# A planned instruction order with refitted prices, whole PSUM tiles as the unit, and another place for the last layer's sums

## The chip, the cores and the metric

The kernel runs on one core of one Trainium2 chip. The core has five engines that run side by side: TensorE (PE) for matmuls, VectorE (DVE), ScalarE (ACT), GpSimd (POOL) and SyncE (SP), which here issues nearly all transfers. Matmuls write PSUM, which has eight banks; everything else lies in SBUF. The metric is the time of one execution on the device in microseconds: 832.44 us is the median of three runs before the change (832.07 to 832.96).

## The reference

The input is q, k, v of 4 batches, 8 heads, 768 tokens and 64 features, and a projection of 64 to 6. Each query and key gets a bucket from the signs of its six projections, and attention is allowed only inside a bucket. The output of attention goes through a two-layer feed-forward net with the activation relu squared.

```python
def _attn_ref(q, k, v, proj):
    q_bits = (np.einsum('bhsd,dk->bhsk', q, proj) > 0)   # k_bits alike
    q_bucket = np.sum(q_bits * powers, axis=-1)
    mask = q_bucket[:, :, :, None] == k_bucket[:, :, None, :]
    scores = np.where(mask, scale * np.matmul(q, k.transpose(0, 1, 3, 2)), -1e9)
    attn = np.exp(scores - np.max(scores, axis=-1, keepdims=True))
    attn = attn / (np.sum(attn, axis=-1, keepdims=True) + 1e-09)
    return np.matmul(attn, v)

def reference(...):                     # x: 3072 x 512
    h = np.maximum(x @ w_in, 0.0)       # w_in: 512 x 2048
    return h * h @ w_out                # w_out: 2048 x 512
```

## The kernel before, in words

**The work.** Numbers are split into two half-precision parts where accuracy needs it, so that one product becomes two or three matmuls. A visit is one batch, one pair of heads and one half (384) of the queries; there are 32. A visit has six units, one for each head and block of 128 queries. `unit` computes the scores pS of 128 queries against 768 keys on TensorE (the matmuls `pS<-A,Q` and `pS<-L,M`; the masks ride in extra rows of the operands), copies them to SBUF on DVE with their maximum (`e<-pS`), takes the exponential on ACT with the sum (`e<-e`), turns the sum into a factor rv (POOL or DVE, and a reciprocal on DVE), and writes the normalised rows as a high part on ACT and a low part on DVE (`hl`). A transposing DMA brings hl to aT. In the first four visits, the plain ones, e is scaled on POOL instead, transposed on TensorE into pT in 32-bit precision and copied out on ACT or DVE. `av` multiplies aT with the values V into pA, which is evicted as two parts xx.

`prep` makes the operands of a head pair: it loads R, splits it into A and L, computes the buckets (`pd`, `bits`, `pc`, M) and stacks the parts with copies inside SBUF (`Q<-L`, `Q<-A`, `A<-A`, `L<-M`, `M<-Q`). `first` does the same for the very first visit in another layout, with K and G loaded side by side and the masks MK and MG out of one PSUM tile pc of three banks.

When the four head pairs of a half of a batch are there, `moe` runs the two dense layers for its 384 tokens; there are eight such stages. For each of 16 slices of 128 hidden units it gathers pm (12 matmuls of 384 columns), evicts it through relu, square and a split into g (high and low part), and adds the slice to po: for each of three token blocks t, three matmuls of 512 columns. po is one PSUM tile of three banks, one for each block. After the last slice the three blocks are evicted into o and sent out. The weights arrive in 32 tiles `raw`, each of which is unpacked on ACT (`top`) and DVE (`f`) and split into win or wo. `verify` looks at the ranges of inputs and weights late in the program; if one were out of range, a second, general program would follow, which does not run here.

**What sets the order.** The functions do not emit instructions. They add operations to a planner, the class `Program`. An operation has one or several ways (engine and form), a rank, and the operations that it depends on. `region` says which part of a tile an operation touches, and `add` makes a dependency where two accesses overlap and at least one writes. For PSUM tiles `region` counts whole banks, so operations in different banks of one tile are independent for the planner. `cost` gives each way a time that the engine is taken and a time until the result is there; for transfers these come from fixed figures and a rate. `forward` then plays the program: at each step the engine that is free first takes the ready operation of best priority; `backward` derives new priorities from that plan, and the best of five plans by its own span is kept. `emit` hands the operations out in the order of this plan, so it fixes the order on every engine, and on SP's queue of transfers. What an instruction really waits for is set below the planner, by the framework that places semaphores from the tiles' accesses. The plan's times play no part on the chip, only its order does.

**Names and lines.** `TRANSPOSES` is the rate for transposing transfers; `TOP_BY`, `LOW_BY`, `RUN` and `ALTERNATE` steer smaller choices. `pS` has two banks, `po` three, `pA`, `pm` and `misc` one each: eight in all. In the profile nearly all instructions carry L427, the line in `emit` that issues single operations, and L424, the one that issues grouped matmuls; they are told apart by their tiles.

Of the kernel before, what the change touches and what calls it, by code (L numbers as in the profile page):

```python
# [23 lines left out]
P = 128  # L24
# [32 lines left out]

WIN_AT, WOUT_AT = (0, 2), 1
# [5 lines left out]
RUN = 18  # L64
CONSTS_BY, WIDE = ("sp", "sp", "sp"), 1
# [16 lines left out]
TRANSPOSES = 165  # L82
# [47 lines left out]
class Program:  # L130
# [25 lines left out]
    def region(view):  # L156
# [5 lines left out]
        if rec.kind == "psum":  # L162
            return 0, 1, f0 // 512, 1 + (f0 % rec.row + size(ap.ap[1:]) - 1) // 512, 0, 0, 0
# [5 lines left out]
    def add(self, *ways):  # L169
# [25 lines left out]
    def cost(key, name, args, kw):  # L195
# [16 lines left out]
        if name.startswith("dma"):  # L212
# [3 lines left out]
            return busy, b / (TRANSPOSES if name == "dma_start_transpose" else 314)  # L216
        if key == "act":
            t = 93 * (isinstance(kw.get("scale"), View) + isinstance(kw.get("bias"), View)) + (51 if "psum" in kinds[:2] else 93) + n / 1.2 + 93 * ("accum_out" in kw)
        elif key == "pool":
            t = 147 + n * (2.1 if args[0].dtype == F32 or args[0].dtype == F32R else 1.88) if name == "tensor_tensor" else 161 + n / 1.2 + 83 * ptr  # L220
        else:
            fast = name in ("tensor_copy", "tensor_scalar") and "psum" not in kinds[:2]
            both = len(args) > 3 and isinstance(args[3], View) and args[3].shape[-1] == 1
            t = 67 + 100 * ("accum_out" in kw) + n / (1.92 if fast else 0.96) + 62 * (ptr and (fast or name == "scalar_tensor_tensor")) + 100 * both
# [93 lines left out]
    def forward(self, prio, near):  # L318
# [7 lines left out]
        free = dict.fromkeys(keys, 0.0)  # L326
        out, dma, dge, held, kind = [], 0.0, 0.0, 0.0, None
# [11 lines left out]
        while True:  # L339
# [109 lines left out]
def run(ctx: ExitStack, tc, kq, v, proj2, w_in, w_out, consts, out, flag):  # L449
# [56 lines left out]
    if fast:  # L506
# [8 lines left out]
        codes = sb([P, 4 * P], BF16, "codes")  # L515
# [148 lines left out]
    def first(hp):  # L664

        K, G = [sb([P, n], F32, name, tag="VV") for name, n in (("K", S), ("G", HS))]
# [3 lines left out]
        MK, MG = sb([P, S], F16, "MK", tag="M"), sb([P, HS], F16, "MG", tag="Q")  # L670
        halves = K[:, 0:HS], K[:, HS:], G
        pd = ps([P, 512], F32, "pd", tag="misc")[:, 0:HS]
        matmuls(*[(pd[32 * n : 32 * n + 32], pj, x) for n, x in enumerate(halves)])
        bits = sb([P, HS], BF16, "bits")
        act.activation(bits[0:96], pd[0:96], AF.Sign, scale=2.0**60, bias=thr[0:96])
# [5 lines left out]
        pr.add((act, "activation", (MG, pc[:, 2], AF.Relu), {"bias": shift}), (dve, "tensor_scalar", (MG, pc[:, 2], 2.0**16, 0.0, ALU.subtract, ALU.max), {}))  # L681
        return K, G, MK, MG

    def side_by_side(st, half, i):

        K, G, MK, MG = st
        c0 = half * HS + i * P
# [51 lines left out]
    def unit(st, half, i, aT, plain, pS=None):  # L739
        c0 = half * HS + i * P  # L740
# [42 lines left out]
    def av(b, hp, half, VV, aTs):  # L783
        pA = ps([P, 512], F32, "pA")[:, 0:HS]
# [8 lines left out]
        xx = xxs[b, half, hp] = sb([P, 2, HS], F16, "xx")  # L793
# [13 lines left out]
    def moe(n, b, half):  # L807
        X = [xxs.pop((b, half, cc)) for cc in range(NCC)]
# [5 lines left out]
        for f in range(NF + 1):  # L814
            if f == NF // 2:
                pr.checked = len(pr.ops)
            if f < NF:
# [3 lines left out]
                for cc in reversed(range(NCC)):  # L821
                    pr.mark = pace()
                    wh = win[:, 0, cc, f * P : (f + 1) * P]
                    wl = win[:, 1, cc, f * P : (f + 1) * P]
                    pe.matmul(pm[:, 0:HS], wh, X[cc][:, 0], start=cc == NCC - 1, stop=False)
                    pe.matmul(pm[:, 0:HS], wh, X[cc][:, 1], start=False, stop=False)
                    pe.matmul(pm[:, 0:HS], wl, X[cc][:, 0], start=False, stop=cc == 0)
                pr.rank, pr.mark = RANK_MOE, None

                g32 = sb([P, HS], F32, "g32", 2)  # L830
                pr.add((act, "activation", (g32, pm[:, 0:HS], AF.Relu), {"scale": HS2 if fast else 2.0**-23}),
                       (dve, "tensor_scalar", (g32, pm[:, 0:HS], HS2 if fast else 2.0**-23, 0.0, ALU.mult, ALU.max), {}))
                square(g32, g32)
                g = gs[f] = sb([P, 2, HS], F16, "g")
# [3 lines left out]
            if f > 0:  # L838
# [4 lines left out]
                if first:  # L843
                    po = ps([P, 3, DM], F32, "po")
                for t in range(3):
# [3 lines left out]
                    pe.matmul(po[:, t], gh, wo[:, 0, m], start=first, stop=False)  # L849
                    pe.matmul(po[:, t], gh, wo[:, 1, m], start=False, stop=False)  # L850
                    pe.matmul(po[:, t], gl, wo[:, 0, m], start=False, stop=last)
# [6 lines left out]
                for t in range(3):  # L858
                    r0 = b * S + half * HS + t * P
                    if grouped and last:  # L860
                        if m == 3:
                            move(acc[:, t], po[:, t], back)
# [170 lines left out]
```

## Time and profile before

| | |
|---|---|
| median of three runs | 832.44 us |
| the profiled execution | 834.86 us |
| its span, first to last instruction | 833.1 us |
| TensorE busy | 794.3 us (95%) |
| ACT busy | 656.6 us (79%) |
| DVE busy | 605.2 us (73%) |
| POOL busy | 72.7 us (9%) |
| DMA, share of 16 engines' span on SP's queue | 77.2% |
| first matmul of a dense layer (pm) | 97.70 us |

The profile is of one execution, with times in us from the first instruction. Busy time of an engine is the union of its instructions. A wait row reads "who waited <- for whom: us in total, times, longest". A timeline row reads "start, duration, engine, line, operation, out<-in, shape, count, and in brackets the idle time before it and what ended it"; instructions of one kind that follow each other are merged into one row. A matmul's duration covers its way through the array, so that matmuls overlap; the step from one to the next is shorter than the duration.

### The profile page before, as it was taken

How to read it: one execution, taken by the hardware profiler on the slowest of the kernel's cores; microseconds unless marked ns; L12 is line 12 of the kernel's file. 1: busy time of each engine (PE TensorE's matmuls, PEld its weight loads, DVE VectorE, ACT ScalarE, POOL GpSimd, SP SyncE). 2: the span in 40 equal slices, each digit the busy share in tenths (PEclk: the TensorE clock that was granted, in tenths of full speed). 3: DMA queues.
4: the chain of work that ended last, by engine and by line, in shares of the span. 5: the costliest groups of instructions: out<-in, count | busy, mean ns of one | idle time of the engine just before them, and what ended most of it. 6: DMA issues, size and time to landing. Idle time of an engine off the chain costs nothing. (4 is left out here: it accounts for less than half of the span.)

```text
span 833.1 us, 14383 instructions
## 1 busy us (share of the span) xinstructions
PE 794.3 (95%) x5001; PEld 430.0 (52%) x5001; DVE 605.2 (73%) x1200; ACT 656.6 (79%) x1238; POOL 72.7 (9%) x175
## 2 busy tenths in 40 slices
PE   7797799999999999999999999999999999999996
PEld 4354355555555554555555545555555554555553
DVE  6888989998999888898879755888889433611110
ACT  5898999998888989888898856888988997334443
POOL 1255200100000010000000000000002000000000
PEclk9999999999999999999999999999999999999999
DMA  8985979999999999999989866988975889501001
GB/s 258 270 223 181 292 188 179 214 176 195 183 202 196 195 188 213 192 181 219 194 188 186 212 165 140 181 143 148 146 133 99 239 290 304 212 1 39 1 1 42
DMA packets 299521, 145.93 MB, mean 175 GB/s; under 512 B 268752, under 2 KB 279344, under 8 KB 299440
## 3 DMA queue, kind: packets, MB, share of 16 engines
q1 hardware_dynamic: 299440, 144.93, 77.2%
q8 instruction: 41, 0.67, 0.3%
q14 instruction: 40, 0.33, 0.1%
HBM read 56.80 MB, written 6.29 MB: 76 GB/s over the span
## 5 line engine op out<-in xcount | busy, mean ns | idle before, releaser
L427 PE MATMUL po<-wo,g 128*128 128x512 f16 x1152 | 296.9, 379 | 5.7 <-ACT o L427 5.7
L427 PE MATMUL pm<-xx,win 128*128 128x384 f16 x1536 | 297.7, 326 | 4.4 <-ACT g L427 2.8
L427 PEld LDWEIGHTS <-win 128*128 128x128 f16 x1536 | 149.9, 98 | 116.6 <-issue 8.0
L427 DVE TENSOR_SCALAR_CACHE_REDUCE e<-pS 128x768 f32<-128x768 f32 x192 | 182.7, 953 | 21.9 <-PE pS L427 17.7
L427 ACT ACTIVATE e<-e,maxes 128x768 f32<-128x768 f32 x192 | 178.2, 929 | 20.7 <-DVE e L427 19.2
L427 DVE SCALAR_TENSOR_TENSOR hl<-e,rv,hl 128x768 f16<-128x768 f32 x168 | 171.0, 1019 | 18.8 <-ACT hl L427 17.8
L427 PEld LDWEIGHTS <-g 128*128 128x128 f16 x1152 | 111.9, 98 | 124.8 <-issue 9.1
L427 ACT ACTIVATE hl<-e,rv 128x768 f16<-128x768 f32 x168 | 154.6, 923 | 6.0 <-DMA aT<-hl 5.2
L427 DVE SCALAR_TENSOR_TENSOR g<-g,g 128x384 f16<-128x384 f32 x121 | 66.9, 553 | 111.8 <-ACT g L427 111.4
L427 ACT ACTIVATE g<-g 128x384 f32<-128x384 f32 (+1 forms) x251 | 129.4, 517 | 6.6 <-PE po L427 2.7
L427 ACT ACTIVATE g<-pm 128x384 f32<-128x384 f32 x127 | 61.2, 482 | 90.3 <-PE pm L427 90.0
L427 PE MATMUL pS<-A,Q 128*128 128x384 f16 x372 | 93.1, 330 | 4.1 <-DVE e L427 2.6
L427 PE MATMUL pS<-L,M 128*128 128x384 f16 x372 | 91.8, 327 | 0.8 <-DMA M<-Q 0.8
L424 PE MATMUL pA<-aT,VV 128*64 128x384 f16 x1008 | 87.2, 327 | 0.0
L427 POOL TENSOR_SCALAR rv<-sums 128x1 f32<-128x1 f32 x136 | 36.8, 271 | 541.7 <-ACT e L427 400.2
L424 PEld LDWEIGHTS <-VV 128*64 128x64 f16 x1008 | 54.7, 110 | 32.9 <-issue 10.0
L427 PEld LDWEIGHTS <-Q 128*128 128x128 f16 x372 | 34.2, 98 | 43.1 <-issue 16.2
L427 DVE TENSOR_SCALAR M<-pc,masks 128x384 f16<-128x384 f32 x64 | 43.0, 672 | 15.4 <-PE pc L427 15.2
L427 PEld LDWEIGHTS <-M 128*128 128x128 f16 x372 | 36.3, 98 | 25.1 <-DMA M<-Q 1.2
L427 ACT ACTIVATION_READ_ACCUMULATOR e<-e,maxes 128x1 f32 x192 | 36.6, 191 | 0.0
L427 DVE SCALAR_TENSOR_TENSOR L<-R,A 128x768 f16<-128x768 f32 x32 | 30.4, 950 | 7.7 <-ACT A L427 7.5
L427 PE MATMUL pT<-unit_f,e 128*128 128x128 f32 x144 | 23.8, 293 | 10.5 <-ACT aT L427 7.7
(82 smaller groups left out, 517.4 us busy)
## 6 DMA issues: line engine op xcount, KB each, us to landing
R<-kq SPq DMA_DIRECT2D x32, 384.0 KB, 3.8
X<-kq SPq DMA_DIRECT2D x32, 384.0 KB, 4.1
raw<-w_in SPq DMA_DIRECT2D x16, 511.8 KB, 5.6
raw<-w_out SPq DMA_DIRECT2D x16, 511.8 KB, 4.9
V<-vp SPq DMA_DIRECT2D x20, 384.0 KB, 5.1
out<-o SPq DMA_DIRECT2D x24, 256.0 KB, 2.7
X<-vp SPq DMA_DIRECT2D x16, 384.0 KB, 4.4
Q<-L SPq DMA_DIRECT2D x32, 96.0 KB, 2.9
```

Source lines behind the costliest of these rows:

```text
L424: ins = q.engine.matmul(*map(real, args), **kw).ins
L427: ins = getattr(q.engine, o.name)(*map(real, o.args), **{k: real(x) for k, x in o.kw.items()}).ins
```

## The change

It has six parts, all in the planner or in what it is told.

1. `region` returns one and the same region for any access to a PSUM tile, so any write to a tile conflicts with any other access to it, whichever bank. Reads of one bank no longer exclude each other in `add`.
2. The prices are other figures: a rate of 190 bytes/ns for transposes, 230 for copies inside SBUF, 325 for loads, each of the latter two with a set-up of 100 ns; 1350 ns from the last byte to the landing (500 for transposes; 910 for both before); a hold of 150 ns in place of 467 on the issuing engine for transposes; 110 ns more for ACT on strided operands; a slower rate for DVE on strided ones and a quicker one between 2-byte operands; 250 ns for POOL on one column; half or 0.7 of the time for pairs of matmuls with 64 rows.
3. `forward` keeps two queues, one for POOL's transfers and one for all others. A transfer is not planned while its queue holds more than `AT_MOST` = 2500 ns of work, and a transfer that is not POOL's blocks its engine until the eighth-last of them has landed (`LANES`). All engines start at 750 ns instead of 0.
4. In `moe`, the last stage's po is no tile of three banks: blocks 0 and 1 lie in a tile of pS's two banks, block 2 in one of pA's. In every stage the eviction of block 1 has DVE as its only way; blocks 0 and 2 keep ACT and DVE.
5. `first` reads 64 rows of codes and bits for MK's two matmuls in place of 96 (the rows left out are zeros in codes), and codes shares memory with g32.
6. Visits and stages take a start and a length of queries in place of a half, so that a batch could be divided unevenly; the table for this, `PARTS`, is empty.

```diff
-TRANSPOSES = 165
+TRANSPOSES, INSIDE, LOADING = 190, 230, 325
+SETUP, LANDING, TURNED, HOLD = 100, 1350, 500, 150
+AT_MOST = 2500
...
         if rec.kind == "psum":
-            return 0, 1, f0 // 512, 1 + (f0 % rec.row + size(ap.ap[1:]) - 1) // 512, 0, 0, 0
+            return 0, 1, 0, 1, 0, 0, 0
...
-                if (w or w2 or rec.kind == "psum") and a0 < p1 and p0 < a1 and b0 < f1 and f0 < b1 and not (fs and fs == bs and (c1 <= g0 or g1 <= c0)):
+                if (w or w2) and a0 < p1 and p0 < a1 and b0 < f1 and f0 < b1 and not (fs and fs == bs and (c1 <= g0 or g1 <= c0)):
...
+            if args[0][0][1].shape[0] == D and len(args) == 2:
+                t *= 0.5 if args[0][0][2].dtype == F32 else 0.7
...
-            return busy, b / (TRANSPOSES if name == "dma_start_transpose" else 314)
+            return busy, b / TRANSPOSES if name == "dma_start_transpose" else SETUP + b / (INSIDE if inside else LOADING)
+        strided = any(isinstance(x, View) and n > 1 and abs(x.ap.ap[-1][0]) > 1 for x in args[:2])
...
-        free = dict.fromkeys(keys, 0.0)
-        out, dma, dge, held, kind = [], 0.0, 0.0, 0.0, None
+        free = dict.fromkeys(keys, 750.0)
+        out, rings, dge, held, kind, lanes = [], [0.0, 0.0], 0.0, 0.0, None, []
...
+            if way[1].startswith("dma") and rings[int(k == "pool")] > t + AT_MOST:
+                heapq.heappush(later[k], (rings[int(k == "pool")] - AT_MOST, i))
+                continue
...
-                dma = max(dma, t + busy + (650 if k != "pool" else 450))
+                ring = int(k == "pool")
+                dma = max(rings[ring], t + busy + (650 if k != "pool" else 450))
                 if o.name == "dma_start_transpose":
-                    o.busy = busy = dma + 467 - t
-                dma += done
-                done = dma + 910 - t
+                    o.busy = busy = dma + HOLD - t
+                shared = min(done, max(0.0, rings[1 - ring] - dma))
+                rings[1 - ring] += shared
+                dma = rings[ring] = dma + done + shared
+                done = dma + (TURNED if o.name == "dma_start_transpose" else LANDING) - t
+                if k != "pool":
+                    lanes.append(t + done)
+                    if len(lanes) >= LANES:
+                        busy = max(busy, lanes[-LANES] + 60 - t)
...
-        codes = sb([P, 4 * P], BF16, "codes")
+        codes = sb([P, 4 * P], BF16, "codes", 2, tag="g32")
...
-        for n in range(3):
-            pe.matmul(pc[:, n], codes[0:96, n * P : (n + 1) * P], bits[0:96], start=True, stop=True)
+        for n, x in enumerate(halves):
+            w = slice(0, 64 if n < 2 else 96) if nq == HS else slice(0, 64) if n < 2 else slice(64, 96)
+            pe.matmul(pc[:, n, 0 : x.shape[1]], codes[w, n * P : (n + 1) * P], bits[w, 0 : x.shape[1]], start=True, stop=True)
...
                 if first:
-                    po = ps([P, 3, DM], F32, "po")
-                for t in range(3):
+                    if fast and (b, q0 + nq) == (B - 1, S):
+                        po = ps([P, 2, 512], F32, "pS"), ps([P, 512], F32, "pA")
+                        po = [po[0][:, 0], po[0][:, 1], po[1]]
+                    else:
+                        po = ps([P, 3, DM], F32, "po")
+                        po = [po[:, t] for t in range(3)]
+                for t in range(nq // P):
...
                         o = sb([P, DM], F32, "o", tag="f")
-                        move(o, po[:, t], back)
+                        move(o, po[t], back, (dve,) if fast and t == 1 else (act, dve, pool))
                         send(out[r0 : r0 + P], o)
```

More of the change, by code (lines that the diff above doesn't have):

```diff
@@ L56 @@
 WHOLE = {0: 0}
+PARTS = {}
 WIN_AT, WOUT_AT = (0, 2), 1
@@ L662, in prep, with first @@
         return out
-    def first(hp):
-        K, G = [sb([P, n], F32, name, tag="VV") for name, n in (("K", S), ("G", HS))]
+    def first(hp, nq):
+        K, G = [sb([P, n], F32, name, tag="VV") for name, n in (("K", S), ("G", nq))]
         for x, w in ((K, T), (G, U)):
@@ L736, in values, with unit @@
         return VV
-    def unit(st, half, i, aT, plain, pS=None):
-        c0 = half * HS + i * P
+    def unit(st, c0, i, aT, plain, pS=None):
         u = pr.rank
@@ L805, in unscaled, with moe @@
         return back
-    def moe(n, b, half):
-        X = [xxs.pop((b, half, cc)) for cc in range(NCC)]
+    def moe(n, b, q0, nq):
+        X = [xxs.pop((b, q0, cc)) for cc in range(NCC)]
         po, gs = None, {}
@@ L848, in moe @@
                     pr.rank, pr.mark = RANK_PE, pace()
-                    pe.matmul(po[:, t], gh, wo[:, 0, m], start=first, stop=False)
-                    pe.matmul(po[:, t], gh, wo[:, 1, m], start=False, stop=False)
-                    pe.matmul(po[:, t], gl, wo[:, 0, m], start=False, stop=last)
+                    pe.matmul(po[t], gh, wo[:, 0, m], start=first, stop=False)
+                    pe.matmul(po[t], gh, wo[:, 1, m], start=False, stop=False)
+                    pe.matmul(po[t], gl, wo[:, 0, m], start=False, stop=last)
                     pr.mark = None
@@ L857, in moe @@
                     acc = sb([P, 3, DM], F32, "acc")
-                for t in range(3):
-                    r0 = b * S + half * HS + t * P
+                for t in range(nq // P):
+                    r0 = b * S + q0 + t * P
                     if grouped and last:
                         if m == 3:
-                            move(acc[:, t], po[:, t], back)
+                            move(acc[:, t], po[t], back)
                         else:
-                            dve.scalar_tensor_tensor(acc[:, t], po[:, t], back, acc[:, t], ALU.mult, ALU.add)
+                            dve.scalar_tensor_tensor(acc[:, t], po[t], back, acc[:, t], ALU.mult, ALU.add)
                         if m == NF - 1:
@@ L926, in run, with pace @@
     step = [0]
-    def pace():
+    def pace(size=1):
         m = step[0]
-        step[0] += 1
+        step[0] += size
         for (u0, m0), (u1, m1) in zip(PACE, PACE[1:]):
@@ L945, in run @@
         F = WHOLE.get(b, H // 2) if fast else H // 2
-        visits += [(b, hp, half) for hp in range(F) for half in range(2)] + [(b, hp, 0) for hp in range(F, H // 2)] + [(b, hp, 1) for hp in range(F, H // 2)]
+        sizes = PARTS.get(b, (HS, HS)) if fast else (HS, HS)
+        parts = [(sum(sizes[:n]), x) for n, x in enumerate(sizes)]
+        visits += [(b, hp, *x) for hp in range(F) for x in parts] + [(b, hp, *x) for x in parts for hp in range(F, H // 2)]
     kept, kept_v = {}, {}
@@ L952, in ready @@
     def ready(visit, rank):
-        b, hp, _ = visits[visit]
+        b, hp, _, nq = visits[visit]
         if fast and visit < WIDE:
             pr.rank = rank
-            wide[visit] = first(hp)
+            wide[visit] = first(hp, nq)
         elif (b, hp) not in kept or not alive(x for st in kept[b, hp] for ab in st for x in ab):
@@ L966, in run @@
     done, u, stages = {}, 0, 0
-    for n, (b, hp, half) in enumerate(visits):
+    for n, (b, hp, q0, nq) in enumerate(visits):
         plain = fast and n in PLAIN_AV
-        aTs = [sb([P, KC, HS], F32, "aT") if plain else sb([P, 2 * KC, HS], F16, "aT") for _ in range(2)]
+        aTs = [sb([P, KC, nq], F32, "aT") if plain else sb([P, 2 * KC, nq], F16, "aT") for _ in range(2)]
         if n in wide:
-            for i in range(3):
-                for aT, pS in zip(aTs, side_by_side(wide[n], half, i)):
+            for i in range(nq // P):
+                for aT, pS in zip(aTs, side_by_side(wide[n], q0 + i * P, i)):
                     pr.rank = u
-                    unit(None, half, i, aT, plain, pS)
+                    unit(None, q0 + i * P, i, aT, plain, pS)
                     u += 1
@@ L977, in run @@
             for aT, st in zip(aTs, kept[b, hp]):
-                for i in range(3):
+                for i in range(nq // P):
                     pr.rank = u
-                    unit(st, half, i, aT, plain)
+                    unit(st, q0 + i * P, i, aT, plain)
                     u += 1
@@ L987, in run @@
         pr.rank = u - 0.5
-        av(b, hp, half, kept_v[b, hp, plain], aTs)
+        av(b, hp, q0, nq, kept_v[b, hp, plain], aTs)
         if n in early:
@@ L991, in run @@
             do(j)
-        done[b, half] = done.get((b, half), 0) + 1
-        if done[b, half] == H // 2:
-            moe(stages, b, half)
+        done[b, q0] = done.get((b, q0), 0) + 1
+        if done[b, q0] == H // 2:
+            moe(stages, b, q0, nq)
             stages += 1
```

43 lines of the change are left out of this document (22 added, 21 removed).

## The prediction

> **What bounds the kernel now.** I read the page's busy rows first, then the stages, then who waits for whom.
>
> ```profile
> PE 794.3 (95%) x5001; PEld 430.0 (52%) x5001; DVE 605.2 (73%) x1200; ACT 656.6 (79%) x1238; POOL 72.7 (9%) x175
> 0.00:98.00 98.00, 74.95 (x485) 43.43 (x486) 79.90 (x177) 80.92 (x162) 36.09 (x53) 0.97 0.83 242
> 98.00:828.00 730.00, 719.35 (x4517) 386.56 (x4515) 525.28 (x1026) 575.66 (x1077) 36.65 (x122) 1.00 0.77 167
> 828.00:834.00 6.00, 0.00 (x0) 0.00 (x0) 0.00 (x0) 0.00 (x0) 0.00 (x0) 0.59 0.16 56
> 97.70 0.32 PE L427 MATMUL pm<-xx,win 128*128 128x384 f16 x1 [1.04 <-ACT xx L427]
> ```
>
> The columns of a stage are PE, PEld, DVE, ACT, POOL busy, granted clock, DMA share, GB/s. There are three stretches. Up to the first dense-layer matmul at 97.70 TensorE idles 98 - 74.95 = 23 us, while DVE and ACT are busy 80 of 98 us each: neither is full, and chains between them, loads and TensorE set the pace. From 98 to 828 us TensorE is busy 719.35 of 730, so the end moves by what is taken out of those 10.65 idle us or out of the first stretch. The last 6 us are the output's landing and the program's end. DVE (525 of 730) and ACT (576 of 730) have room to follow a TensorE that is 1% quicker.
>
> ```profile
> PE pT L427 <- ACT aT L427: 7.7, 8, 2.2
> PE po L427 <- ACT o L427: 5.7, 8, 0.9
> PE pc L427 <- ACT bits L427: 3.0, 2, 2.8
> PE pm L427 <- ACT g L427: 2.8, 5, 1.0
> PE pS L427 <- DVE e L427: 2.6, 4, 1.4
> ```
>
> The second row is over half of the 10.65 us: matmuls of the second layer, po, wait eight times for the eviction of po into o. The end of the timeline shows what such a wait is:
>
> ```profile
> 820.81 3.40 PE L427 MATMUL po<-wo,g 128*128 128x512 f16 x15
> 824.25 0.60 ACT L427 ACTIVATE o<-po 128x512 f32<-128x512 f32 x1 [1.64 <-PE po L427]
> 824.90 0.81 PE L427 MATMUL po<-wo,g 128*128 128x512 f16 x3 [0.69 <-ACT o L427]
> 825.74 0.60 ACT L427 ACTIVATE o<-po 128x512 f32<-128x512 f32 x1 [0.90 <-PE po L427]
> 826.39 0.59 PE L427 MATMUL po<-wo,g 128*128 128x512 f16 x2 [0.69 <-ACT o L427]
> 827.02 0.60 ACT L427 ACTIVATE o<-po 128x512 f32<-128x512 f32 x1 [0.68 <-PE po L427]
> ```
>
> po is one tile of three banks, one bank for each of three token blocks. Block 0's sums end, its eviction runs, and block 1's matmuls, which write another bank, start only when the eviction is over. The planner before counts a bank as the unit, so it is free to place an eviction between two blocks' matmuls; the program that is built waits as if the tile were the unit.
>
> **The change part by part.**
>
> *The tile as unit.* With the new region of PSUM tiles every eviction comes behind all nine closing matmuls in the planner's order, since it now depends on all of them. So the eight waits go. One costs its 0.69 us of idle and the refill of the pipeline: fifteen matmuls take 3.40 us, which with 0.38 for a matmul alone is (3.40 - 0.38) / 14 = 0.216 apiece, so each restart costs 0.38 - 0.216 = 0.16 more. Eight waits: 5.7 + 8 x 0.16 = **7.0 us**. All eight lie in the TensorE order after 98 us, so all of it is on the path. What is late next is the eviction itself, since block 0 is now emptied after block 2's sums, 6 x 0.216 = 1.3 us later, with the next layer's first po behind it. Cover for that is next layer's first pm and the attention matmuls: at an earlier border the second and third eviction already ran late.
>
> ```profile
> 422.16 0.60 ACT L427 ACTIVATE o<-po 128x512 f32<-128x512 f32 x1 [0.56 <-PE po L427]
> 422.81 0.59 PE L427 MATMUL po<-wo,g 128*128 128x512 f16 x2 [0.69 <-ACT o L427]
> 423.44 0.60 ACT L427 ACTIVATE o<-po 128x512 f32<-128x512 f32 x1 [0.68 <-PE po L427]
> 424.75 0.59 ACT L427 ACTIVATE o<-po 128x512 f32<-128x512 f32 x1
> ```
>
> Here ACT still evicts at 425.34, 1.9 us after the last po matmul, and no row above says that po waited for it. Without that cover one eviction per border, 0.6 us, would come back. The Trainium skill, page "PSUM — Partial Sum Buffer", section "Summary: rules for kernel authors", says that reading PSUM while a matmul runs is in order if the matmul targets a different bank. By that rule none of these waits is needed, the whole-tile figure would only forbid a legal overlap, and this term would be 0 or a small loss; the 0.69 us rows show the wait in another bank all the same, and they decide.
>
> *Block 1 on DVE, the last layer in the banks of pS and pA.* Eight evictions go to DVE. There is no such row; the nearest ones are
>
> ```profile
> L427 ACT ACTIVATE o<-po 128x512 f32<-128x512 f32 x24 | 13.9, 591 | 7.1 <-PE po L427 7.0
> L427 DVE TENSOR_SCALAR MK<-pc 128x384 f16<-128x384 f32 x2 | 1.0, 553 | 0.1
> L427 DVE SCALAR_TENSOR_TENSOR xx<-pA,xx x32: 536/552/560, 43.2 to 713.8; 128x384 f16<-128x384 f32 x32
> L427 DVE TENSOR_SCALAR_CACHE_REDUCE e<-pS x192: 937/952/959, 13.8 to 648.4; 128x768 f32<-128x768 f32 x192
> 766.43 0.38 PE L427 MATMUL po<-wo,g 128*128 128x512 f16 x1
> ```
>
> So between 0.59 and 553 x 512 / 384 = 0.74 us; I take 0.7. Eight of them are 6 us of DVE's 525 against 4.7 us less on ACT: nothing while TensorE is the bound; if DVE were the late one, 0.7 us a border. In the last layer blocks 0 and 1 are emptied by ACT and DVE side by side while block 2, in a tile of its own, computes for 0.65 us; ACT's 0.6 is over when block 2 ends, and block 2's eviction follows as now. So the tail shifts by the two waits at 824.90 and 826.39, which are among the eight, and nothing is added. pS and pA are free there: their last reads start at 648.4 and 713.8 us, and the last layer's po begins at 766.43.
>
> *The first visit.* The same tile rule acts on pc, three banks again:
>
> ```profile
> 9.82 0.32 PE L427 MATMUL pc<-bits,codes 96*128 96x384 bf16 x1
> 10.41 0.56 ACT L427 ACTIVATE MG<-pc,masks 128x384 f16<-128x384 f32 x1
> 11.02 0.48 PE L427 MATMUL pc<-bits,codes 96*128 96x384 bf16 x2
> 11.62 1.02 DVE L427 TENSOR_SCALAR MK<-pc 128x384 f16<-128x384 f32 x2
> ```
>
> The second and third pc could follow the first at 9.98; they start at 11.02, behind ACT's MG. Planned as one tile, the two MK come up to 1.0 us earlier, and so does the first full pS. Bounds 0 and 1.0; I take **0.5**, since the chain of loads beside it is not shortened. Fewer rows in these matmuls (64 in place of 96) change no duration that a row shows, the move of codes into g32's memory is covered by 86 us between codes' last use at 11.5 and the first g32 after 97.70, and the new parameters for uneven parts are unused (PARTS is empty): all 0.
>
> *Refitted prices, queue limit, SP's eight outstanding transfers.* These change no instruction, only the order on all engines and on SP's queue. How near the old and new prices lie to the trace:
>
> ```profile
> R<-kq SPq DMA_DIRECT2D x32, 384.0 KB, 3.8
> raw<-w_in SPq DMA_DIRECT2D x16, 511.8 KB, 5.6
> Q<-L SPq DMA_DIRECT2D x32, 96.0 KB, 2.9
> L427 SPq DMA_TRANSPOSE aT<-hl x168: 1382/1468/3233, 116.5 to 698.7; - x168
> DMA to landing us min/median/max: 3.6/3.9/6.4
> L427 ACT ACTIVATE top<-raw 128x512 f16<-128x512 bf16 x32 | 25.0, 780 | 4.1 <-DMA raw<-w_out 2.2 <-DMA raw<-w_in 1.5
> L427 POOL TENSOR_SCALAR rv<-sums 128x1 f32<-128x1 f32 x136 | 36.8, 271 | 541.7 <-ACT e L427 400.2 <-DVE hl L427 114.6 <-DVE rv L427 9.9
> ```
>
> On an empty queue a load of 384 KB was planned to land after 475 + 650 + 393216/314 + 910 = 3.29 us and is now after 3.78 (row 3.8); a transpose of the same bytes after 4.59, now 3.87 (row 3.9); its hold on SP was 1.77, now 1.45 (row 1.47); a strided top 520 ns, now 630 (row 780); rv 162, now 250 (row 271). Q<-L goes from 2.52 to 3.18 (row 2.9), an overshoot as large as the old undershoot. So the plan gets nearer the chip in five of six. What this is worth shows no row; bounds come from the idle time that is left. After 98 us that is 10.65 - 5.7 = 5 us at most. In the first stretch loads held the engines up as follows:
>
> ```profile
> ACT A L427 <- DMA R<-kq: 4.6, 2, 3.0
> ACT top L427 <- DMA raw<-w_out: 2.0, 2, 1.6
> ACT top L427 <- DMA raw<-w_in: 1.5, 3, 0.6
> PE pS L427 <- DMA A<-A: 1.3, 1, 1.3
> ```
>
> together 9.4 us. If all that overlapped with nothing else, 9.4 would be the best case; half, 5, is a fair upper gain, as some of these waits lie beside each other's work. A new order can as well create such waits: four plain visits stand in this stretch, and a load that lands late in each, by the mean 4.6 / 2 = 2.3 us of the A row, costs 9. Between -5 and +9 I take **-0.5**, near zero, because the prices are nearer but an order of 7000 operations is rearranged as a whole.
>
> Sum: -7.0 - 0.5 - 0.5 = -8.0 us. The profiled execution took 834.86 us with a span of 833.1, 1.8 us around it; so 826.9 for it. It lies 2.4 above the median 832.44 of the runs; set against the median, the forecast is **824.4 us**.
>
> **The rivals.**
>
> *The first stretch gains too.* Holding back transfers until a queue is under 2.5 us lets R and the copies pass the weights' raw tiles, and half of the 9.4 us goes: 824.4 - 4.5, some 820 and below to 814. For it: ACT idles 17 of 98 us. Against: eight of the pT waits are on ACT's aT, not on loads.
>
> *The wait changes its place.* All three evictions now begin together after the last closing matmul and the next layer's po finds its tile not yet empty. Then of the eight waits only the two in the last layer are gained, 2 x 0.85 = 1.7, with 0.5 from the first visit: 830.2. Against it: the 1.9 us lag above without a wait.
>
> *Slower.* The queue limit with eight outstanding transfers puts weight tiles behind the attention's copies, and their splitting meets the first dense layer. Each raw tile costs ACT 780 ns for top alone, and DVE its share; fifteen of the 32 tiles that move from before 97.70 to behind it while pm waits on them are 11.7 us of ACT in TensorE's way. It decides when the first pm comes later than about 106 us, 8 us being what the other terms gain; with those 11.7 lost the time is 836. For it: DMA is at 0.83 of its capacity in this stretch, so the order of loads matters. Against: ACT and DVE have 17 us spare each. The Trainium skill, page "TensorE: Matmul & The Clock Gate", section "What's actually happening", adds that TensorE drops to half clock after an idle window of about 3.4 us; the longest idle in the waits above is 2.8 us and the mean clock of the stretch 0.97, so longer gaps would cost somewhat more than their length.
>
> *No effect.* The eight waits go but the new order brings as many of the pm and pS kind (2.8 and 2.6 us here, 5.4 together, plus a later start by 2 us): 832.
>
> **How the numbers follow.** Forecast, with its own range 820 to 829: 0.50. First stretch gains too: 0.20. Wait changes place: 0.10, of which 0.08 counts as faster. No effect: 0.06. Slower: 0.14. About 0.2% (1.7 us) is what a measurement of this kernel can tell from no change. Faster: 0.50 + 0.20 + 0.08 = 0.78; same: 0.06 + 0.02 = 0.08; slower 0.14. The range leaves out the lowest part of the first rival and most of the slower case: 815 to 834.
>
> **What would show it right or wrong.** Right: the row of po waiting for ACT o is gone or under 1 us; the closing po matmuls of each layer run nine in a row; DVE shows eight rows of o at about 0.7 us; the last eviction starts some 1.7 us sooner after the layer's first matmul; the three pc matmuls of the first visit stand together; TensorE idle from the first pm to the end falls from 10.65 us to about 5. The first pm lies at 97 us, give or take 4. Wrong: a first pm beyond 106 us, a new row of po waiting on DVE o, or new waits of pm and pS above 8 us together would make it fail; a first pm at 92 us would make it too cautious.

## The result, and the profile after

The changed kernel takes 826.58 us, the median of four runs (825.57 to 828.41), against 832.49 before: a ratio of 0.9931 with a 95% interval of 0.991 to 0.9952, so 5.9 us less, and the interval leaves no change out. The forecast was 824.4, 8 us less; the time lies in its range, and the gain is three quarters of what was forecast. The profiled execution took 828.41 us with a span of 826.6; the spans of the two profiled executions differ by 6.5 us. Each of the two took longer than the median of its kernel, by 2.4 us before and 1.8 after.

First the busy row of the changed kernel's page, and its groups' row of the first dense-layer matmul, pm (count, least, mean and longest duration, first start and last end). Lines of the code have moved: L445 answers to the L427 of before, L442 to L424.

```profile
PE 796.9 (96%) x4998; PEld 430.3 (52%) x4998; DVE 604.1 (73%) x1223; ACT 650.3 (79%) x1229; POOL 87.1 (11%) x161
```

```profile
L445 PE MATMUL pm<-xx,win x1536: 322/326/337, 93.5 to 815.2; 128*128 128x384 f16 x192
```

Its stages, up to 98 us, from there to 820, and the rest left out (length, busy time of PE, PEld, DVE, ACT and POOL, granted clock, DMA share, GB/s):

```profile
0.00:98.00 98.00, 81.29 (x505) 45.87 (x506) 81.62 (x183) 83.33 (x168) 43.42 (x58) 0.97 0.82 249
98.00:820.00 722.00, 715.27 (x4495) 384.47 (x4492) 521.87 (x1040) 566.33 (x1062) 43.71 (x103) 1.00 0.79 167
```

In the first 98 us TensorE is busy 81.29 - 74.95 = 6.3 us longer than before, above all because the first pm starts at 93.5 and not at 97.7. From 98 us on it idles 722 - 715.27 = 6.7 us, where it was 10.65.

The waits of TensorE from the first pm to 815 us, in the changed kernel and then in the kernel before (who waited, for whom: us in total, times, longest). The last layer's two waits of po, 1.4 us, lie behind 815 in the kernel before; the changed kernel has none there:

```profile
PE pS L445 <- DVE e L445: 3.8, 5, 1.2
PE po L445 <- ACT g L445: 1.6, 3, 0.8
PE pm L445 <- ACT xx L445: 1.6, 1, 1.6
PE pA L442 <- DMA aT<-hl: 0.6, 1, 0.6
PE pm L445 <- DVE xx L445: 0.6, 1, 0.6
PE pm L445 <- ACT g L445: 0.4, 1, 0.4
PE po L445 <- DVE g L445: 0.2, 1, 0.2
```

```profile
PE po L427 <- ACT o L427: 4.3, 6, 0.9
PE pm L427 <- ACT g L427: 2.8, 5, 1.0
PE pm L427 <- ACT xx L427: 1.5, 2, 1.0
PE pS L427 <- DVE e L427: 0.3, 1, 0.3
```

The row of po waiting for an eviction is gone, all of it. But the scores pS wait for DVE to empty their banks, 3.8 us where it was 0.3, and po waits for g. All rows together are 8.9 + 1.4 = 10.3 us before and 8.8 in the changed kernel (10.5 and 9.3 in e5 and e6 below, the two kernels on another chip): of the 5.7 us that went, the new order has 4.2 elsewhere. Here are a border between two dense layers and the end of the program, in the changed kernel's timeline:

```profile
195.28 1.89 PE L445 MATMUL po<-wo,g 128*128 128x512 f16 x8
197.21 0.60 ACT L445 ACTIVATE o<-po 128x512 f32<-128x512 f32 x1 [1.37 <-PE po L445]
197.84 0.69 DVE L445 TENSOR_SCALAR o<-po 128x512 f32<-128x512 f32 x1 [0.70 <-ACT o L445]
199.53 0.58 ACT L445 ACTIVATE o<-po 128x512 f32<-128x512 f32 x1
...
819.05 1.24 PE L445 MATMUL pA<-wo,g 128*128 128x512 f16 x5
819.25 0.60 ACT L445 ACTIVATE o<-pS 128x512 f32<-128x512 f32 x1 [2.01 <-PE pS L445]
819.88 0.69 DVE L445 TENSOR_SCALAR o<-pS 128x512 f32<-128x512 f32 x1 [2.05 <-ACT o L445]
820.33 0.60 ACT L445 ACTIVATE o<-pA 128x512 f32<-128x512 f32 x1 [0.48 <-PE pA L445]
```

No eviction stands between the closing matmuls any more. They are nine in a row only in the last layer, though; in the other seven layers other matmuls stand among them. The last eviction starts 59.1 us after the last layer's first po, where it was 60.6, so 1.5 sooner for the forecast's 1.7. DVE takes block 1, for 0.69 us, but it starts when ACT's eviction of block 0 has ended (197.21 + 0.60, then 197.84; 819.25 + 0.60, then 819.88), though the two read different banks.

### The profile page after: what moved, and what is told of

It reads as the page before. It is cut to its first block, busy times and chain, and to the rows that moved or that the text cites. A ratio compares the mean times of both kernels' runs of the same rounds, so it can differ in the third digit from the quotient of the medians.

```text
span 826.6 us, 14311 instructions
## 1 busy us (share of the span) xinstructions
PE 796.9 (96%) x4998; PEld 430.3 (52%) x4998; DVE 604.1 (73%) x1223; ACT 650.3 (79%) x1229; POOL 87.1 (11%) x161
## 4 chain that ended last, share of the span: by engine, by line
PE 72%; ACT 11%; DVE 7%; DMA 6%; issue 4%; POOL 0%; SPq 0%; ACTq 0%; DVEq 0%; POOLq 0%
PE pm L445 24%; PE po L445 20%; PE pS L445 13%; PE pA L442 9%; DMA aT<-hl 6%; ACT e L445 3%; ACT hl L445 2%; DVE e L445 2%; DVE hl L445 2%; PE pd L442 1%; PE pA L445 1%; ACT g L445 1%; ACT aT L445 1%; ACT top L445 1%; PE pc L445 1%
## 5 line engine op out<-in xcount | busy, mean ns | idle before, releaser
L445 PE MATMUL pm<-xx,win 128*128 128x384 f16 x1536 | 301.8, 326 | 2.6 <-ACT xx L445 1.6
L445 PE MATMUL po<-wo,g 128*128 128x512 f16 x1008 | 274.5, 379 | 1.8 <-ACT g L445 1.6
L445 PEld LDWEIGHTS <-win 128*128 128x128 f16 x1536 | 150.1, 98 | 114.3 <-issue 4.8
L445 ACT ACTIVATE e<-e,maxes 128x768 f32<-128x768 f32 x192 | 178.4, 930 | 27.0 <-DVE e L445 26.3
L445 DVE TENSOR_SCALAR_CACHE_REDUCE e<-pS 128x768 f32<-128x768 f32 x192 | 182.5, 951 | 14.4 <-PE pS L445 12.7
L445 DVE SCALAR_TENSOR_TENSOR hl<-e,rv,hl 128x768 f16<-128x768 f32 x168 | 169.9, 1015 | 27.7 <-ACT hl L445 26.4
L445 PEld LDWEIGHTS <-g 128*128 128x128 f16 x1152 | 111.5, 98 | 122.3 <-issue 4.6
L445 ACT ACTIVATE hl<-e,rv 128x768 f16<-128x768 f32 x168 | 154.9, 925 | 19.5 <-DMA aT<-hl 14.4
L445 DVE SCALAR_TENSOR_TENSOR g<-g,g 128x384 f16<-128x384 f32 x116 | 64.3, 554 | 109.5 <-ACT g L445 100.7
L445 ACT ACTIVATE g<-g 128x384 f16<-128x384 f32 (+1 forms) x249 | 128.4, 516 | 7.4 <-PE po L445 3.9
L445 ACT ACTIVATE g<-pm 128x384 f32<-128x384 f32 x128 | 61.7, 482 | 88.6 <-PE pm L445 87.3
L445 PE MATMUL pS<-A,Q 128*128 128x384 f16 x372 | 94.2, 327 | 5.4 <-DVE e L445 4.9
L445 PE MATMUL pS<-L,M 128*128 128x384 f16 x372 | 94.1, 327 | 0.0
L442 PE MATMUL pA<-aT,VV 128*64 128x384 f16 x1008 | 87.9, 327 | 0.6 <-DMA aT<-hl 0.6
L445 POOL TENSOR_SCALAR rv<-sums 128x1 f32<-128x1 f32 x110 | 36.0, 328 | 471.7 <-ACT e L445 420.3
L442 PEld LDWEIGHTS <-VV 128*64 128x64 f16 x1008 | 55.4, 110 | 32.8 <-issue 9.9
L445 PEld LDWEIGHTS <-Q 128*128 128x128 f16 x372 | 34.5, 98 | 43.3 <-issue 18.9
L445 PEld LDWEIGHTS <-M 128*128 128x128 f16 x372 | 36.3, 98 | 24.3 <-issue 0.9
L445 DVE TENSOR_SCALAR M<-pc,masks 128x384 f16<-128x384 f32 x64 | 42.8, 669 | 4.6 <-PE pc L445 4.4
L445 ACT ACTIVATION_READ_ACCUMULATOR e<-e,maxes 128x1 f32 x192 | 37.0, 193 | 0.0
L445 PE MATMUL pS<-wo,g 128*128 128x512 f16 x96 | 34.9, 379 | 0.0
L445 DVE RECIPROCAL rv<-rv 128x1 f32<-128x1 f32 x192 | 29.7, 158 | 2.5
```

Of the source, the lines that this page charges most:

```text
L442: ins = q.engine.matmul(*map(real, args), **kw).ins
L445: ins = getattr(q.engine, o.name)(*map(real, o.args), **{k: real(x) for k, x in o.kw.items()}).ins
```

## The experiments

Three theories stood against each other. Theory 1, the forecast's: the eight waits are worth 7 us, and nearly all of the gain is theirs. Rival A: a stall taken out there comes back as another. Rival B: the gain lies in the first stretch. Theory 2 came after e1 to e4: the waits' worth comes off only with a second engine evicting and the last layer in banks of its own. Rival C: the gain is one favourable order among many.

The table puts all runs side by side. Three quantities go with the ratio. The first pm is its start in the profiled execution. "Beyond the steps" is the time from there to the start of the last matmul, less the number of matmuls of each kind times the step of its kind in steady work (0.162 us for pm, pS and pc, 0.216 for po and pt, 0.085 for pA, 0.097 for pd); some records are missing, so it is good to about 1 us. "End" goes from the start of the last matmul to the end of the span. The runs e1 to e12 came in three sets, each on another chip and with its own median of before: 833.78, 833.59 and 832.67 us.

| kernel | ratio to before, 95% interval | first pm | beyond the steps | end |
|---|---|---|---|---|
| before, two traces | 1 | 97.7, 97.3 | 17.9, 20.2 | 6.5, 6.4 |
| changed, first chip | 0.9931, 0.991 to 0.9952 | 93.5 | 16.0 | 6.7 |
| e6, changed again | 0.9925, 0.9901 to 0.9949 | 93.4 | 15.9 | 7.2 |
| e1, waits alone | 0.9983, 0.9964 to 1.0002 | 94.1 | 14.5 | 7.8 |
| e7, waits and DVE | 0.9965, 0.9949 to 0.9981 | 98.1 | 14.4 | 8.7 |
| e9, waits, DVE, last layer | 0.9964, 0.9953 to 0.9975 | 95.4 | 12.9 | 7.2 |
| e2, tile unit alone | 1.0055, 1.0034 to 1.0076 | 103.5 | 15.1 | 8.5 |
| e3, prices and queue alone | 0.9964, 0.9948 to 0.998 | 96.1 | 16.5 | 9.1 |
| e4, changed but bank unit | 0.9977, 0.996 to 0.9994 | 92.8 | 16.7 | 8.9 |
| e8, changed but shared po | 0.9971, 0.9958 to 0.9985 | 96.1 | 15.3 | 9.5 |
| e10, landing 1340 | 0.9996, 0.9983 to 1.001 | 96.3 | 16.1 | 9.0 |
| e11, landing 1360 | 0.9946, 0.993 to 0.9962 | 96.5 | 13.7 | 6.8 |
| e12, no queue limit | 0.997, 0.9951 to 0.9988 | 98.0 | 13.9 | 8.7 |

**e1: the waits alone.** The plan of before is kept; when an eviction of po comes up, the layer's remaining po matmuls are emitted first.

```diff
+        seen = {}
         for i in out:
+            for j in sorted(self.closing.get(i, ())) + [i]:
+                seen.setdefault(j)
+        for i in seen:
             o = self.ops[i]
...
+                        pr.closing[len(pr.ops)] = sums     # all po matmuls of the layer
                         move(o, po[:, t], back)
```

> The kernel before with its plan, prices and ways untouched; only where the plan puts an eviction of po between the closing matmuls of its layer, the remaining po matmuls of that layer are emitted ahead of it. Theory 1 (the eight waits of po on ACT o lie on TensorE's path and cost 7.0 us): about 825.5 us, the row of po waiting for ACT o gone, the first pm still near 97.7. Rival A (TensorE's stalls are conserved: what is taken out there comes back within the next layer as waits on ACT g or DVE e): 829 to 832, with new rows of pm and pS of some 4 us. Rival B (the gain of the changed kernel came from the first stretch alone): 832.

Measured: 831.81 against 833.78 us, 2.0 less by the medians, 1.4 by the ratio, whose interval reaches to no change. Theory 1 falls in its size. The eight waits between closing matmuls are gone, but at three of the seven borders the next layer's first po waits. The row of the waits, and one of these borders in the timeline:

```profile
PE po L432 <- ACT o L432: 2.7, 3, 1.2
```

```profile
693.10 0.59 PE L432 MATMUL pt<-sq,ones 128*128 128x512 bf16 x2
693.79 1.06 ACT L432 ACTIVATE o<-po 128x512 f32<-128x512 f32 x2
694.90 1.02 PE L432 MATMUL po<-wo,g 128*128 128x512 f16 x4 [1.21 <-ACT o L432]
```

ACT evicts the three blocks one after another among its other work, and the next layer's first po waits for the third. With the refills these are 2.7 + 3 x 0.16 = 3.2 us of the 7.0. Waits of pS for DVE e grew too, from 0.3 to 1.5 us. At the end all three evictions come after the last matmul, and the end is 1.3 us longer:

```profile
815.65 4.26 PE L432 MATMUL po<-wo,g 128*128 128x512 f16 x19
819.96 1.57 ACT L432 ACTIVATE o<-po 128x512 f32<-128x512 f32 x3 [2.72 <-PE po L432]
```

**e2: the tile as unit alone**, in the kernel before.

```diff
-            return 0, 1, f0 // 512, 1 + (f0 % rec.row + size(ap.ap[1:]) - 1) // 512, 0, 0, 0
+            return 0, 1, 0, 1, 0, 0, 0
...
-                if (w or w2 or rec.kind == "psum") and a0 < p1 ...
+                if (w or w2) and a0 < p1 ...
```

> The kernel before with one part of the change: PSUM tiles counted whole, with reads free of each other; old prices, old queue, old place of po. Theory 1: 825 to 826, as the waits go, and the first pm at 96.7 to 97.7 (up to 1.0 from the first visit). Rival A (a new order makes new waits): the row of po gone, but 828 to 832. Rival B: no change in the first stretch and 832.

Measured: 837.96 us, 0.55% slower. The waits of po on o are gone as planned, and the new order loses more than that before the dense layers begin: the first pm starts 5.8 us later than before. The transposes pT wait 12.9 us for ACT to copy pT out to aT, where it was 7.7 (5.2 in e5); but TensorE's idle time from 4 us to the first pm is no longer than before, 19.0 and 20.0 us, so these waits are not what the start costs. TensorE is busy 6.8 us longer there, with 499 matmuls where it was 478 and a granted clock of 0.93 where it was 0.96. The row of the waits and the row of pm:

```profile
PE pT L427 <- ACT aT L427: 12.9, 13, 2.1
```

```profile
L427 PE MATMUL pm<-xx,win x1536: 322/326/337, 103.5 to 823.4; 128*128 128x384 f16 x192
```

**e3: the prices and the queue alone.** `cost`, `forward` and the constants are those of the changed kernel, `region`, `first` and `moe` those of before.

```diff
-TRANSPOSES = 165
+TRANSPOSES, INSIDE, LOADING = 190, 230, 325
+SETUP, LANDING, TURNED, HOLD = 100, 1350, 500, 150
+AT_MOST = 2500
...
```

> The kernel before with the other large part: the refitted prices, the limit on queued transfers and the eight outstanding ones, with banks as PSUM's unit and the old place of po. Theory 1: the waits of po on ACT o stay (8 to 16 of them, 6 to 12 us) and the time is 832, give or take 3. Rival B (the first stretch is what the prices improve, and it is all of the gain): first pm at 93.5 and 826 to 828.5.

Measured: 830.88 us, a ratio of 0.9964. Seven waits of po on ACT o are there, 4.8 us, as theory 1 had it, and the time is faster all the same, by 3.0 us (1.7 to 4.3 by the interval): inside theory 1's range and outside rival B's. The first pm at 96.1 is 1.4 earlier than the mean of before's two.

**e4: the changed kernel with banks as the unit again** (e2's diff the other way round).

> The changed kernel with one part undone: banks as PSUM's unit again. Theory 1: the waits of po on ACT o or DVE o come back in the first seven layers, two each at most, some 6 to 12 of them, and the time is 826.6 + 5 to 10 = 832 to 836 with the first pm still near 93.5. Rival A: the waits come back but others go, 827 to 829. Rival B: 826.6.

Measured: 831.49 us, a ratio of 0.9977. Both theory 1 and rival B miss. Only two waits of po on ACT o came back, 1.4 us; the rest of the 3.8 us that e4 is slower than the changed kernel does not lie in them, and its first pm is the earliest of all, in an execution whose granted clock was 1.00 from 4 us to there.

**e5 and e6: the two kernels again**, on one other chip, with no edit.

> The kernel before, unchanged: it shows what two sets of runs of one kernel differ by on this chip, and gives a trace of it here. Every theory: a ratio of 1.000 within its interval; if two equal kernels differ by over 0.2% here, differences of the parts below that are not told apart.

> The changed kernel, unchanged, on the chip of this call. If the gain does not hang on the chip: ratio 0.991 to 0.995 again, with the first pm 3 to 5 us earlier than in the trace of the kernel before from the same call. If the earlier first pm was an accident of the granted clock in two traces: the difference of the first pm is under 2 us where both have the same clock up to there.

Measured: e5 against the other runs of the same kernel 1.0001, with an interval of 0.9984 to 1.0018; e6 828.1 us, a ratio of 0.9925. The gain is the same on another chip. The first pm is at 97.3 and 93.4, and the granted clock does not explain it: the trace of before has one stretch at half clock there (64.6 to 68.0), the changed one two (14.4 to 17.8 and 82.7 to 86.1). On the three later chips single runs of before spread from 830.8 to 837.5; on the first, four had 832.07 to 832.96, and the profiled one 834.86.

**e7: e1 with DVE for block 1**, at its place in the plan of before.

```diff
+            if i in self.on_dve:                    # the eviction of block 1
+                o.queue, o.name, o.args, o.kw = o.ways[0][:4]
```

> As e1_waits_only (plan and prices of before, closing po matmuls kept together), and the eviction of block 1 done by DVE at its place in that plan. In e1 three borders showed po waiting for ACT's third eviction, 3.2 us in all with the refills. Theory 2 (the waits' 7.0 us come off in full only with a second engine evicting): those three waits fall to under 1 us together, TensorE loses about 8 us beyond its steps after the first pm (14.5 before, 11.4 in e1), and the time is 5 to 7 us under before, ratio 0.992 to 0.994. Rival A (stalls conserved): the waits move on to DVE o, g or e and the ratio stays at 0.997 to 0.999 as in e1.

Measured: 830.89 us, a ratio of 0.9965, 2.9 us less than before. Between the two theories: the border waits fall from 2.7 to 1.8 us and do not go, and the end is 2.2 us longer than before. (The expectation counts TensorE's loss another way; its 14.5 and 11.4 us are 17.9 and 14.5 in the table.)

**e8: the changed kernel without its fourth part.**

```diff
-                    if fast and (b, q0 + nq) == (B - 1, S):
+                    if False:
...
-                        move(o, po[t], back, (dve,) if fast and t == 1 else (act, dve, pool))
+                        move(o, po[t], back)
```

> The changed kernel without its fourth part: the last layer's po in the three-bank tile again, and each eviction free to take ACT or DVE. Theory 2: the planner gives most evictions to ACT, waits of po on ACT o of the border kind come back at two to four borders, 2 to 4 us, and the tail is up to 0.7 us longer; ratio to the kernel before 0.996 to 0.999. If the fourth part does nothing: the same ratio as the changed kernel in this call.

Measured: 831.17 us, a ratio of 0.9971 beside 0.9925 for the changed kernel on the same chip; the intervals do not touch. But the border waits that theory 2 names are not there: its waits of TensorE have no row of po on o. The planner gave all 24 evictions to ACT, and at the end the three stand behind the last matmul:

```profile
817.32 4.26 PE L445 MATMUL po<-wo,g 128*128 128x512 f16 x19
821.62 1.58 ACT L445 ACTIVATE o<-po 128x512 f32<-128x512 f32 x3 [2.50 <-PE po L445]
```

The last eviction ends at 823.20, 2.0 us after the last matmul's start at 821.20; in the changed kernel it is 1.0 us (820.93 and 819.91). That is what the last layer's place is worth here, 1 us. What else the two traces differ by is the first pm, 2.7 us later, and a second wait of 1.8 us at the program's end, of which more below.

**e9: e7 with the last layer's po in the banks of pS and pA**, swapped when instructions are emitted, so that the plan stays that of before.

```diff
+        if self.rec.split:                          # po of the last layer
+            x, path = self.rec.split(path[0][1][0][1]), path[1:]
```

> As e7_waits_and_dve, still with the plan and prices of before, and the last layer's po placed in the banks of pS (blocks 0 and 1) and pA (block 2) when the instructions are emitted. Theory 2 (in e7 the last layer lost what its two waits had cost, since all three evictions and the three outputs came after its last matmul): from the last matmul to the end 6.5 to 7.2 us in place of 8.67, and the time 1.5 to 2.5 us under e7, ratio to the kernel before 0.993 to 0.995. If the end is as long for another reason: the same 0.9965 as e7.

Measured: 829.56 against 832.67 us, a ratio of 0.9964. The end is 7.2 us as expected and "beyond the steps" the smallest of all, 12.9. The time did not follow: e7 and e9 have the same ratio, though their intervals leave room for the 1.5 us by which the ends differ. All that is mechanical in the change, without a new order, is worth 3.0 us (2.1 to 3.9 by the interval).

**e10 and e11: a price moved by ten nanoseconds**, and **e12: no limit on queued transfers**, each in the changed kernel.

```diff
-SETUP, LANDING, TURNED, HOLD = 100, 1350, 500, 150
+SETUP, LANDING, TURNED, HOLD = 100, 1340, 500, 150     # e10; 1360 in e11
...
-AT_MOST = 2500
+AT_MOST = 10**9                                        # e12
```

> The changed kernel with one price moved by less than any row can tell: transfers land 1340 ns after their last byte in place of 1350. Theory 2 (the gain is made of the waits, the last layer's place and the nearer prices): the same ratio as the changed kernel, 0.990 to 0.995. Rival C (a good part of the gain is one favourable order among many, and any small move of a price draws another): a ratio outside that, 0.995 to 1.001, with the first pm moved by 2 us or more or with new waits.

> As the run before, with 1360 ns. Theory 2: 0.990 to 0.995. Rival C: 0.995 to 1.001; if this and the run before differ from the changed kernel or from each other by more than 0.3%, differences of that size between the parts of the change are no measure of the parts.

> The changed kernel without the limit on queued transfers (the planner may queue any amount). Theory 2: loads pass ahead of the attention's copies in the first stretch, the first pm is 1 to 4 us later than 93.4 and the ratio to the kernel before is 0.994 to 0.999. If the limit does nothing: the ratio of the changed kernel. Rival C: anything within what the two runs before show.

Measured: 832.91, 828.66 and 831.15 us; ratios of 0.9996, 0.9946 and 0.997. This is rival C. No row of a trace tells 1340 from 1350 ns, and yet the smaller figure gives back the whole gain. Part of that goes with the granted clock: over whole executions it was 0.991 to 0.995 in e10 and 0.994 to 0.999 in the changed kernel, and where both had 0.994 or 0.995, e10's three spans are 828.5 to 829.0 us and the changed kernel's five 826.2 to 829.1. Between e10 and e11 it is not the clock: at 0.991 to 0.993 nine spans of e10 are 829.3 to 833.3 us, and the six of e11 825.8 to 827.4. The three have the changed kernel's waits of po (none on o at the closing matmuls; e11 has one of 0.4 us at a border) and its place for the last layer; what differs is the order as a whole, first of all in the first stretch:

```profile
L445 PE MATMUL pm<-xx,win x1536: 322/326/337, 96.3 to 818.1; 128*128 128x384 f16 x192
```

```profile
L445 PE MATMUL pm<-xx,win x1536: 322/326/337, 96.5 to 815.9; 128*128 128x384 f16 x192
```

e10 loses 2.8 us there and 2.3 at the end against the changed kernel's first trace, 5.1 of its 5.2 us of longer span (831.8 and 826.6). e12's ratio lies between those of e10 and e11, so the limit by itself is not told apart from such a draw, and neither are e2, e3, e4 and e8 wherever they differ by less than 0.5%.

## Why the prediction was right, and where it was not

**The tile as unit, 7.0 us.** The mechanism was right: the row of po waiting for ACT o is gone, no eviction interrupts the closing matmuls, and the eight waits had been there in both traces of before (5.7 and 6.0 us). The size was not. The step that failed is "all of it is on the path", and with it the cover that was claimed for what is late next. Taken out alone, with nothing else moved, the waits gave 1.4 us (e1), 2.9 with DVE for block 1 (e7) and 3.0 with the last layer's place (e9). In e1 3.2 us came back where the forecast's rival had put them, at the next layer's first po; I had excluded that from one border with a lag of 1.9 us, and three others had none. In the changed kernel those border waits do not appear, but pS waits for DVE e 3.5 us more, and all waits together fell by 1.5 us. "Beyond the steps" went from 17.9 and 20.2 to 16.0 and 15.9, some 3 us, not 7. TensorE's idle time after 98 us fell to 6.7 us, not to about 5.

**Block 1 on DVE.** The price was right (0.69 us for the estimated 0.7). That ACT and DVE empty blocks 0 and 1 side by side was wrong: in the changed kernel no two evictions of one PSUM tile overlap, at none of the eight places. Evictions of two tiles do: the last one, of pA, starts at 820.33, and DVE's of pS ends at 820.57. At the end this cost nothing, because block 2 is a tile of its own and ended last, as forecast; the end grew by 0.3 to 0.7 us, where nothing was forecast.

**The first visit, 0.5 us.** The three pc matmuls stand together now, as forecast, and it brought next to nothing, in part for the same reason:

```profile
10.33 0.75 PE L445 MATMUL pc<-bits,codes 64*128 64x384 bf16 x3
11.12 0.56 DVE L445 TENSOR_SCALAR MK<-pc 128x384 f16<-128x384 f32 x1 [3.50 <-PE pc L445]
11.71 0.58 ACT L445 ACTIVATE MG<-pc,masks 128x384 f16<-128x384 f32 x1 [1.43 <-DVE MK L445]
12.33 0.56 DVE L445 TENSOR_SCALAR MK<-pc 128x384 f16<-128x384 f32 x1 [0.65 <-ACT MG L445]
12.35 0.33 PE L442 MATMUL pS<-MK,MG 64*128 64x384 f16 x1 [0.71 <-ACT MG L445]
```

MK, MG and MK again wait for each other, though each has a bank to itself, and the first masked pS starts at 12.35, where it was 12.49. The first pc itself starts 0.5 us later than before, at 10.33 for 9.82. The chain of evictions that was serial through TensorE before is serial through the tile now.

**The prices and the queue, 0.5 us.** This term was mis-sized most. e3, which has it alone, gained 3.0 us, and in the changed kernel's traces the first pm came 4.2 us earlier (3.9 on the other chip), near the early edge of the forecast's 97 give or take 4. A single execution also moves there: before, e5, e1, e7 and e9 have one and the same order up to the first pm, and it started at 97.7, 97.3, 94.1, 98.1 and 95.4; against their mean of 96.5 the changed kernel's two are 3 us early. The rival that expected an earlier first pm gave loads as the reason. ACT's waits on loads in the first stretch did go, from 8.1 us to none, while ACT's wait for the first projection grew from 3.5 us and DVE's for the constants from 1.4; these are the changed kernel's rows of the two:

```profile
ACT bits L445 <- PE pd L442: 7.4, 2, 6.9
DVE codes L445 <- DMA sgn_f<-consts: 3.5, 2, 3.1
```

But on ACT e10, e11 and e12 have no more than 0.4 us of waits on loads either, and their first pm is at 96.3, 96.5 and 98.0. So it is not enough that these waits go. More can be read from the stage from 4 us to the first pm, here of before, the changed kernel, e10 and e11 (columns as above):

```profile
4.00:97.70 93.70, 73.67 (x478) 42.35 (x476) 77.83 (x164) 79.34 (x161) 35.89 (x49) 0.96 0.84 247
4.00:93.50 89.50, 76.78 (x478) 42.93 (x476) 76.12 (x164) 78.25 (x160) 43.22 (x54) 0.96 0.83 252
4.00:96.28 92.28, 79.12 (x478) 43.38 (x476) 76.44 (x164) 79.96 (x163) 43.58 (x53) 0.94 0.84 250
4.00:96.53 92.53, 78.36 (x478) 43.26 (x476) 77.42 (x168) 80.09 (x164) 42.87 (x49) 0.93 0.87 261
```

TensorE idles 93.70 - 73.67 = 20.0 us there before, and 12.7, 13.2 and 14.2 in the other three. The five traces with the order of before have 18.6 to 22.4 us and e2, with the old prices, 19.0; the seven with the new prices and the limit, of six orders, have 11.9 to 14.7 (the changed kernel twice, e3, e4, e8, e10, e11), and e12, without the limit, 17.7. So the shorter idle time goes with the prices and the limit, as far as one or two traces of each order can tell, and not with one order among many. The first pm does not follow it in full: for the same 478 matmuls TensorE is busy 2.3 us longer in e10 and 1.6 in e11 than in the changed kernel, at a granted clock of 0.94 and 0.93 for 0.96. That the clock is the reason is not shown; e7 and e12 had 1.00 and started at 98.1 and 98.0.

**The sum.** The 8.0 forecast and the 5.9 measured are near each other because two errors offset, and that is luck: the waits with DVE and the last layer's place were worth some 3 us in place of 7 (e9), and the prices, the queue and the order that they make some 3 in place of 0.5 (e3). That 3.0 and 3.0 add up to the 5.9 and 6.2 us of the changed kernel is no proof, since its neighbours at 1340 and 1360 ns lie 0.5% apart. What stays open is which of its thousands of places make this order quicker than theirs, and what lets the granted clock differ between them.

## What to carry to other kernels

A wait between two engines on one tile is worth its length only if the next buffer in the chain is free in time: take the wait out alone, with the order held, before counting it. When an order is made by a planner, move one of its figures by an amount without meaning and time that first; here ten nanoseconds either way gave 0.9946 and 0.9996, so a part of such a change can be judged only where its effect is larger than that, or at a place that a trace shows. Compare the granted clock of the executions too. Sums that end a program are better off in more than one tile, so that two engines can empty them at once; here the program's end was 1 to 1.5 us shorter by it (e8, and e9 against e7). A tile for each of the three blocks was not tried.

## What the runs showed of the hardware that was not expected

The program's end has a second length. In the changed kernel SyncE waits once after the last output, in e10 twice:

```profile
SPq L462 <- SPq L462: 3.2, 1, 3.2
```

```profile
SPq L462 <- SPq L462: 5.2, 2, 3.2
```

The second wait is 2.0 us there. By a count of SyncE's records, the traces with 867, 858 and 849 of them (both kernels twice, e1, e7, e9, e11) have no second wait of more than 0.1 us, and those with 865, 846, 845, 844 and 836 (e2, e12, e8 and e10, e3, e4) are held up there by 0.9 to 2.7 us. On each of the three later chips there are traces with it and without it, but each kernel that has it was traced once only. In four of the six with it a packet of instructions is fetched in the last 0.9 us of the span, and in none of the eight others. That the fetch of instructions makes the wait was not tried. It is part of the differences between the variants: the changed kernel is without it, e10 has it, and that is 2 of the 5 us between them.

The granted clock halves for 3.4 us at a time (once for 6.8 in e2 and in e11), and how often it does so differs between executions of one order: in the first stretch of before, e5, e1, e7 and e9 two times, once, never, never and once. In the trace of before one such stretch began at 30.4 us, though between 4 us and there TensorE was never idle for longer than 2.8 us. It isn't the reason for a late first pm by itself, since e1 and e7, both without it, started at 94.1 and 98.1.
